# Moving the store of converted weight rows from the sync queue to GpSimd's queue

## The chip, the cores and the metric

The kernel runs on one core of a Trainium2 chip. The core has five engines that run side by side and wait for one another through semaphores: PE (TensorE, matmuls and transposes), DVE (VectorE), ACT (ScalarE), POOL (GpSimd) and SP (SyncE, which here only issues transfers). Each engine takes its instructions strictly in the order in which the program was built. The metric is the device time of one execution in microseconds (us), as the median of a few runs.

## The reference, cut to what matters

Attention with local windows and a few global tokens makes `x` of 2304 rows; a dense layer pair follows; its result goes through a soft mixture of experts.

```python
x = attn_out.transpose(0, 2, 1, 3).reshape(B * S, H * D)   # 2304 x 512
h = x @ w_in                                               # 512 x 2048
g = np.maximum(0.01 * h, h)
y = g @ w_out                                              # w_out: 2048 x 512
logits = y @ phi                                           # phi: 512 x 32
d = softmax of logits over the rows; slot_input = d.T @ y
slot_out = per expert: maximum(slot_input @ w1, 0) @ w2
out = softmax of logits over the columns @ slot_out
```

`w_in` and `w_out` arrive as 64-bit floats, which the kernel reads as pairs of 32-bit words.

## The kernel before

`g @ w_out` is never formed for all rows. The kernel needs `w_out` twice: early as `w_out @ phi` (the tile `pmat`, with which logits come straight from `g`), and late, at about 430 us, as the 32-bit weights that turn the summed rows into `slot_input`. So a phase of the program, from about 75 to 140 us, converts `w_out` in 16 chunks of 128 rows, here called chunk 0 to chunk 15. For each chunk:

- SP loads the raw words into a ring of four buffers (`rraw`, L233; chunks 0 to 3 come in halves into other buffers).
- `convert` makes 32-bit floats: two scalings on ACT (L251 and L250, the second into a fresh buffer `wo`), two bit operations on DVE (L253, L257), an integer add on POOL (L261).
- SP stores `wo` to a scratch tensor `wo_f` in HBM (L338), from where four transfers fetch it back at 324 us (L1063).
- PE transposes `wo` in four pieces (`wotp`, L345), ACT copies the result to `wt` (L347), and PE multiplies it with `phi` (`ptps`, L354). After every fourth chunk the product is copied (DVE, `pv`, L359), transposed (PE, L360) and stored in `pmat` (ACT, L361).

There are three `wo` buffers: L250 of one chunk needs the store and the transposes of the third chunk before it. The one PSUM buffer of `wotp` makes each group of transposes wait for the copy to `wt` of the chunk before.

The same stretch holds other work. Attention for the second batch runs score matmuls (`sc`, L434), masked maxima on DVE (L446), four exponentials for each half on ACT (L454), transposes (`etp`, L473), and the product with the values (`po`, L493; DVE scales it into `xn`, L501). The first dense layer runs matmuls (`hp`, L689), whose results are transposed (`gtp`, L726), copied (`gT`, L728, on ACT or DVE in turn) and multiplied with `pmat` (`lg`, L887). The buffer of `xn` for the second batch lies where the raw and `wo` buffers lay, so L501 also waits for the last stores of `wo`.

What order these have on an engine is decided when the program is built: the code names the pieces in a merged list, and a scheduler that plays the program against its own idea of durations then fixes one order for each engine. A changed instruction can therefore change the order of others.

Of the kernel before, what the change touches and what calls it, by code (L numbers as in the profile page):

```python
# [20 lines left out]
def kernel(  # L21
# [15 lines left out]
    nc = tc.nc  # L37
# [4 lines left out]
    P = 128  # L42
# [27 lines left out]
    with tc.tile_pool(name="id", bufs=1) as idp:  # L70
# [6 lines left out]
        out=s44[:, 0, :], in_=ident.rearrange("p (g s) -> p s g", g=4), axis=AX.X, op=ALU.add  # L77
# [58 lines left out]
    for r in range(2):  # L136
        nc.gpsimd.affine_select(
            out=em4[:, r, :], in_=em4[:, r, :], compare_op=ALU.is_ge, fill=0.0,
# [3 lines left out]
            out=em4[:, r, :], in_=em4[:, r, :], compare_op=ALU.is_ge, fill=0.0,  # L142
# [147 lines left out]
    wo_f = dr.tile([FF, DM], F32, name="wo_f") if w_out.dtype == I64 else w_out  # L290
# [25 lines left out]
    def p_items():  # L316
# [16 lines left out]
        def conv_(c, j):  # L333
            wo = pb.tile([P, 512], F32, tag="wo", name="wo", bufs=3)
            for h in range(2) if c == 0 else (None,):
                wout_s.next(wo if h is None else wo[:, 256 * h:256 * h + 256])
            if wo_f is not w_out:
                nc.sync.dma_start(out=wo_f[512 * j + P * c:512 * j + P * c + P, :], in_=wo)  # L338
            wos.append(wo)

        def chunk(c, j):
# [20 lines left out]

        seq_ = [(c, j) for c in range(4) for j in range(4)]
        items.append((0.0, lambda: conv_(0, 0)))
        for n, (c, j) in enumerate(seq_):
            if n + 1 < len(seq_):
                items.append((0.2, lambda a=seq_[n + 1]: conv_(*a)))
            items.append((0.5, lambda c=c, j=j: chunk(c, j)))
            if j == 3:
                items.append((1.2, lambda c=c: prod(c)))  # L370
# [691 lines left out]
    for n, t in enumerate(wo2):  # L1062
        nc.sync.dma_start(  # L1063
            out=t, in_=wo_f[512 * n:512 * n + 512, :].rearrange("(k p) f -> p k f", p=P)
# [193 lines left out]
    for t0 in range(0, NTT, 4):  # L1258
        n = min(4, NTT - t0)
        pt = bank("sc", "ctp", 2)  # L1260
        for t in range(n):
# [7 lines left out]
            out=dst, in0=dst, scalar=odd, in1=pt[:, 0:P * n], op0=ALU.mult, op1=ALU.add  # L1269
# [21 lines left out]
    for m, (c0, c1) in enumerate(((0, 256), (256, 384), (384, 512))):  # L1291
        W = c1 - c0
        sop = bank(("po", "sm", "tp")[m], "sop", 1 if m < 2 else 2)[:, 0:W]
        for k in range(KF):
# [9 lines left out]
            out=so[:, c0:c1], in0=so0[:, c0:c1], in1=sop, op=ALU.add  # L1304
# [3 lines left out]
        if m == 0:  # L1308
# [3 lines left out]
            out=sst[64:128, c0:c1], in0=sp[64:128], in1=sst[64:128, c0:c1], op=ALU.subtract  # L1312
# [4 lines left out]
        for n, ts in enumerate(order2):  # L1317
# [14 lines left out]
            if len(ts) == 1:  # L1332
# [3 lines left out]
                    out=out.rearrange("(b r) c -> b r c", b=B)[:, 0:SG, c0:c1], in_=ob  # L1336
                )
            else:
# [5 lines left out]
                    out=out[r0:r0 + G * P, c0:c1].rearrange("(t p) c -> p t c", p=P), in_=ob  # L1344
# [36 lines left out]
```

## Time and profile before

| | |
|---|---|
| median of 3 runs | 497.02 us (496.87 to 497.91) |
| the profiled execution | 496.2 us |
| its span, first to last instruction | 494.5 us |
| PE busy | 463.5 us, 94% of the span |
| DVE, ACT, POOL busy | 275.0, 234.3, 160.3 us |
| mean granted clock of TensorE | 0.979 of full speed |

The profiled execution took 1.7 us more than its span. PE is busy nearly all the time, so what matters is the few places where PE stands idle, and whatever adds or removes such a place. Busy time of the other engines counts only where PE waits for them.

### The profile page before, as it was taken

To read this page: it belongs to the slowest core of one execution; us is meant where nothing else is said; L and a number is where in the kernel's file an instruction comes from. 1 tells how busy PE (TensorE), PEld (TensorE's weight loads), DVE (VectorE), ACT (ScalarE), POOL (GpSimd) and SP (SyncE) were. 2 spreads that over 40 slices of the span, in tenths; PEclk is the share of its full clock that TensorE was granted. 3 is DMA by queue.
4 is the path that set the end of the run, shared out by engine and by line. 5 is a ranking of instruction groups with operands and counts; after the bars stand their busy time and mean duration, and the time that the engine had idled before them with its cause. 6 is when DMAs were issued, how large, how long until landed. Compare 5 with 4: busy or idle time off the path is not lost.

```text
span 494.5 us, 13438 instructions
## 1 busy us (share of the span) xinstructions
PE 463.5 (94%) x5323; PEld 322.0 (65%) x5323; DVE 275.0 (56%) x886; ACT 234.3 (47%) x680; POOL 160.3 (32%) x281
## 2 busy tenths in 40 slices
PE   7867889999989999999999999999999999999993
PEld 5645668666766657776777676777777777533463
DVE  4585888498547776556554656427666511413332
ACT  4776899588655345543435444234444432201122
POOL 2044887342400113460615243243667700000000
PEclk9986899999999999999999999999999999999998
DMA  9989598599457655334250231169420079999977
GB/s 177 223 200 267 183 292 313 185 304 311 150 143 144 143 118 93 85 76 129 60 106 1 60 60 45 44 220 405 150 78 2 23 266 357 364 397 371 305 237 214
DMA packets 118362, 90.23 MB, mean 182 GB/s; under 512 B 75356, under 2 KB 100764, under 8 KB 118300
## 3 DMA queue, kind: packets, MB, share of 16 engines
q1 hardware_dynamic: 115628, 88.33, 61.8%
q10 hardware_dynamic: 2672, 1.05, 0.8%
q8 instruction: 42, 0.69, 0.6%
q14 instruction: 20, 0.16, 0.1%
HBM read 76.68 MB, written 8.65 MB: 173 GB/s over the span
## 4 chain that ended last, share of the span: by engine, by line
PE 78%; DVE 4%; ACT 4%; DMA 1%; issue 1%; POOL 0%; ACTq 0%; DVEq 0%; POOLq 0%
PE hp L689 38%; PE gtp L726 4%; PE ehp L1221 3%; PE sc L434 3%; PE up L810 3%; PE po L493 3%; PE lg L740 2%; PE etp L473 2%; PE sop L1297 2%; PE sop L1275 1%; PE gpo L579 1%; PE wotp L345 1%; PE qTp L390 1%; PE kTp L390 1%; PE xtp L659 1%; PE gl L519 1%
## 5 line engine op out<-in xcount | busy, mean ns | idle before, releaser
L689 PE MATMUL hp<-wi,xxh 128*128 128x512 f32 x512 | 167.2, 408 | 1.2 <-ACT xxh L665 1.2
L689 PEld LDWEIGHTS hp<-wi,xxh 128*128 128x128 f32 x512 | 91.8, 190 | 28.2 <-issue 8.2
L717 POOL COPY g<-gb 32x256 f32<-32x256 f32 x206 | 82.7, 401 | 82.6 <-DVE gb L708 55.5
L689 PE MATMUL hp<-wi,xxl 128*128 128x512 f32 x256 | 101.0, 396 | 0.0
L696 ACT ACTIVATE g<-hp 128x512 f32<-128x512 f32 x60 | 35.3, 595 | 56.2 <-PE hp L689 54.2
L454 ACT ACTIVATE se<-se,nmx 128x128 f32<-128x128 f32 x128 | 49.6, 390 | 21.5 <-DVE nmx L452 21.4
L689 PEld LDWEIGHTS hp<-wi,xxl 128*128 128x128 f32 x256 | 48.3, 189 | 12.5 <-issue 1.7
L200 POOL COPY vw<-vw 32x1664 f32<-32x1664 f32 x10 | 15.8, 1575 | 78.3 <-DMA vw<-in_v_g_dram 34.9
L446 DVE CUSTOM_DVE_ANT_0 se<-sc,mask 128x128 f32<-128x128 f32 x128 | 28.9, 284 | 12.1 <-PE sc L434 12.0
L261 POOL TENSOR_TENSOR wn<-wn,rraw 128x512 int32<-128x512 int32 x16 | 22.8, 1435 | 34.5 <-DVE wn L257 33.0
L708 DVE STREAM_TRANSPOSE gb<-g 128x512 f32<-128x512 f32 x32 | 22.2, 702 | 19.3 <-ACT g L696 14.0
L434 PE MATMUL sc<-kw,qT 64*32 64x128 f32 x1024 | 29.2, 283 | 0.8 <-DVE mx L446 0.4
L493 PE MATMUL po<-vw,eT 128*32 128x64 f32 x1024 | 24.2, 232 | 3.5 <-issue 2.1
L261 POOL TENSOR_TENSOR wo<-wo,rraw 128x512 int32<-128x512 int32 x12 | 16.0, 1332 | 31.7 <-DVE wo L257 7.2
L434 PEld LDWEIGHTS sc<-kw,qT 64*32 64x32 f32 x1024 | 19.8, 109 | 8.9 <-issue 5.3
L493 PEld LDWEIGHTS po<-vw,eT 128*32 128x32 f32 x1024 | 18.4, 116 | 10.2 <-issue 7.4
L477 DVE COPY eT<-etp 128x512 f32<-128x512 f32 x28 | 18.7, 684 | 9.9 <-PE etp L473 9.9
L454 ACT ACTIVATION_READ_ACCUMULATOR se<-se,nmx 128x1 f32 x128 | 24.1, 188 | 0.0
L473 PE MATMUL etp<-identr,se 128*128 128x128 f32 x128 | 22.4, 296 | 0.2
L405 DVE COPY kw<-kT 128x672 f32<-128x672 f32 x32 | 19.8, 653 | 3.1 <-ACT kT L394 2.7
L251 ACT ACTIVATE rraw<-rraw 128x512 int32<-128x512 uint32 x28 | 18.7, 673 | 4.3 <-DMA rraw<-in_moe_w_out_dram 3.1
L473 PEld LDWEIGHTS etp<-identr,se 128*128 128x128 f32 x128 | 15.8, 146 | 6.3 <-ACT se L454 2.3
(232 smaller groups left out, 777.9 us busy)
## 6 DMA issues: line engine op xcount, KB each, us to landing
ew<-in_moe_w_dram SPq DMA_DIRECT2D x23, 1024.0 KB, 9.5
rraw<-in_moe_w_in_dram SPq DMA_DIRECT2D x16, 512.0 KB, 5.5
vw<-in_v_l_dram SPq DMA_DIRECT2D x60, 112.0 KB, 3.2
rraw<-in_moe_w_out_dram SPq DMA_DIRECT2D x12, 512.0 KB, 6.7
ew<-in_moe_w_dram SPq DMA_DIRECT2D x9, 512.0 KB, 9.2
ew<-in_moe_w_dram SPq DMA_DIRECT2D x17, 256.0 KB, 5.5
wo_f<-wo SPq DMA_DIRECT2D x16, 256.0 KB, 3.2
vn<-in_v_l_dram SPq DMA_DIRECT2D x4, 1024.0 KB, 6.3
```

The lines of the kernel that those rows point to most:

```text
L261: nc.gpsimd.tensor_tensor(out=di, in0=di, in1=m, op=ALU.add)
L405: nc.vector.tensor_copy(kw[:, :, 0:96], src)
L434: last_a[0] = nc.tensor.matmul(bks[e][32 * u:32 * u + 32, P * T:P * T + P], qt[64 * e:64 * e + 64, 32 * U:32 * U + 32], kw[win(U) // (NW / ...
L446: nc.vector.tensor_tensor_reduce(out=s[:, T, :], in0=bk[:, P * T:P * T + P], in1=mask[:, 0 if T == 0 else 2 if T == NT - 1 else 1, :], sca ...
L454: exp_last[0] = nc.scalar.activation(out=s[:, T, :], in_=s[:, T, :], func=AF.Exp, bias=nmx[:, e, T:T + 1], accum_out=sm[:, T, e:e + 1],).ins
L473: last_a[0] = nc.tensor.transpose(pt[:, P * T:P * T + P], es[e][:, T, :], ident).ins
L493: last_a[0] = nc.tensor.matmul(pov[32 * u:32 * u + 32, T, e, :], ets[e][:, 32 * U:32 * U + 32], vw[:, win(U), e, :], start=True, stop=True ...
L689: nc.tensor.matmul(hp, a[:, k, :], w[c][:, k, :], start=(k == 0 and n == 0), stop=(k == KD - 1 and n == 2),)
L696: nc.scalar.activation(out=gs, in_=hp, func=AF.Prelu, alpha=0.01)
L708: nc.vector.transpose(out=gb[:, f % 2], in_=gs)
L717: copy(dst[32 * c:32 * c + 32, :, a], src[32 * a:32 * a + 32, :, c])
L726: nc.tensor.transpose(pt[:, P * c:P * c + P], g[:, o:o + P], ident)
```

## The change

One call goes to another engine. The store of each converted chunk is issued from POOL, whose add completes the chunk, instead of from SP.

```diff
             if wo_f is not w_out:
-                nc.sync.dma_start(out=wo_f[512 * j + P * c:512 * j + P * c + P, :], in_=wo)
+                nc.gpsimd.dma_start(out=wo_f[512 * j + P * c:512 * j + P * c + P, :], in_=wo)
             wos.append(wo)
```

Sixteen transfers of 256 KB leave SP's queue and stand in POOL's. There each follows the add of its own chunk and waits for that add; only chunks 1 and 2 are stored together, behind the add of chunk 2. No other POOL instruction changes its place. On SP the loads that stood behind a store now follow one another, and some raw loads stand ahead of attention's loads where they stood behind.

The scheduler also puts other engines' work in another order between chunk 8 and chunk 15. In the rows below, one row counts a score or value matmul once where the trace shows it as two.

PE around chunks 8 to 10 (before with -, the change with +): the score matmuls of the second batch's first heads are `sc_1555` and `sc_1556`.

```order
-L345 MATMUL wotp<-identr,wo 128x128 x4
-L434 MATMUL sc_1555<-kw,qT 32x128 x16
+L434 MATMUL sc_1555<-kw,qT 32x128 x15
+L345 MATMUL wotp<-identr,wo 128x128 x4
+L434 MATMUL sc_1555<-kw,qT 32x128
 L390 MATMUL qTp<-identr,qn 128x128 x4
 L360 MATMUL ptps<-identr,pv 128x128
-L345 MATMUL wotp<-identr,wo 128x128 x4
 L434 MATMUL sc_1556<-kw,qT 32x128 x16
-L354 MATMUL ptps<-wt,phis 32x128 x2
+L354 MATMUL ptps<-wt,phis 32x128
+L345 MATMUL wotp<-identr,wo 128x128 x4
```

The transposes of chunk 8 moved behind most of `sc_1555`, those of chunk 9 behind `sc_1556`. Further on, those of chunk 10 moved behind four `hp` matmuls, and those of chunk 11 behind twenty more.

PE at the end of the conversion, from the transposes of chunk 13 on, before:

```order
L345 MATMUL wotp<-identr,wo 128x128 x4
L354 MATMUL ptps<-wt,phis 32x128
L493 MATMUL po<-vw,eT 32x64 x15
L434 MATMUL sc_1981<-kw,qT 32x128 x16
L493 MATMUL po<-vw,eT 32x64 x4
L345 MATMUL wotp<-identr,wo 128x128 x4
L354 MATMUL ptps<-wt,phis 32x128
L493 MATMUL po<-vw,eT 32x64 x7
L434 MATMUL sc_1982<-kw,qT 32x128 x16
L345 MATMUL wotp<-identr,wo 128x128 x4
L354 MATMUL ptps<-wt,phis 32x128 x14
```

And in the change, from the value matmuls just ahead of chunk 13 on:

```order
L493 MATMUL po<-vw,eT 32x64 x9
L345 MATMUL wotp<-identr,wo 128x128 x4
L354 MATMUL ptps<-wt,phis 32x128
L434 MATMUL sc_1981<-kw,qT 32x128 x16
L354 MATMUL ptps<-wt,phis 32x128
L345 MATMUL wotp<-identr,wo 128x128 x4
L434 MATMUL sc_1982<-kw,qT 32x128 x16
L354 MATMUL ptps<-wt,phis 32x128
L345 MATMUL wotp<-identr,wo 128x128 x4
L354 MATMUL ptps<-wt,phis 32x128 x13
L726 MATMUL gtp<-identr,g_860 128x128 x4
L887 MATMUL lg<-gT,pmat 32x128 x3
```

The value matmuls and a block of `hp` that stood between these chunks now stand ahead of chunk 13; chunk 12's transposes moved from ahead of that block to behind it, 16 value matmuls, the transpose L360 and the 9 shown above ahead of chunk 13's. Behind the last `lg` row shown, the change has the second `gtp` of this tile, which before stood ahead of it.

ACT at the same place, before:

```order
L361 ACTIVATE pmat<-ptps 128x128
L250 ACTIVATE wo<-rraw 128x512
L347 COPY wt<-wotp 128x512 x2
L454 ACTIVATE se,sm<-se,nmx 128x128 x4
L347 COPY wt<-wotp 128x512
L454 ACTIVATE se,sm<-se,nmx 128x128 x4
L728 COPY gT<-gtp 128x512 x2
```

And in the change:

```order
L250 ACTIVATE wo<-rraw 128x512
L361 ACTIVATE pmat<-ptps 128x128
L347 COPY wt<-wotp 128x512
L250 ACTIVATE wo<-rraw 128x512
L347 COPY wt<-wotp 128x512
L454 ACTIVATE se,sm<-se,nmx 128x128 x8
L347 COPY wt<-wotp 128x512
L728 COPY gT<-gtp 128x512 x2
```

The last copy to `wt` stood behind the first four exponentials and now stands behind all eight; the first scaling of chunk 15 (the last L250) moved behind the copy of chunk 13. On DVE the second bit operation of chunk 15 (L257) moved behind the four masked maxima of `sc_1981`.

## Rows read from the trace of the kernel before

**Rows 1.** Stretches: start:end, length, busy us of PE, PEld, DVE, ACT, POOL.

```profile
104.00:120.00 16.00, 14.46 (x213) 10.26 (x213) 15.04 (x48) 13.10 (x35) 6.21 (x5) 1.00 1.10 301
131.00:142.00 11.00, 9.36 (x181) 6.91 (x179) 5.09 (x25) 6.70 (x23) 2.59 (x2) 1.00 0.41 121
200.00:300.00 100.00, 100.00 (x1375) 72.38 (x1373) 56.53 (x229) 44.30 (x160) 37.11 (x76) 1.00 0.32 69
```

**Rows 2.** Waits of PE, 60 to 170 us: total, times, longest.

```profile
PE gtp L726 <- DVE gT L728: 1.3, 1, 1.3
PE wotp L345 <- POOL wo L261: 0.7, 1, 0.7
...
PE sc L434 <- DVE mx L446: 0.4, 1, 0.4
```

**Rows 3.** Waits of SP's queue, 60 to 145 us, the longest.

```profile
SPq L338 <- POOL wo L261: 23.0, 10, 3.3
```

**Rows 4.** Instructions on tile wo: shortest/median/longest ns, first and last start.

```profile
L253 DVE TENSOR_SCALAR wo<-wo x20: 280/426/1289, 75.5 to 133.3; 128x512 uint32<-128x512 uint32 x12, 128x256 uint32<-128x256 uint32 x8
L338 SPq DMA_DIRECT2D wo_f<-wo x16: 319/338/1523, 80.7 to 136.9; - x16
L250 ACT ACTIVATE wo<-rraw x12: 660/686/706, 87.9 to 132.6; 128x512 f32<-128x512 f32 x12
L257 DVE SCALAR_TENSOR_TENSOR wo<-rraw,wo x12: 689/692/693, 89.8 to 133.8; 128x512 uint32<-128x512 uint32 x12
L261 POOL TENSOR_TENSOR wo<-wo,rraw x12: 1288/1304/1552, 90.8 to 134.8; 128x512 int32<-128x512 int32 x12
```

**Rows 5.** The stores of line L338, from issue to landing.

```profile
DMA to landing us min/median/max: 2.0/3.2/6.2
```

**Rows 6.** Timeline of SP, the last store: start, length.

```profile
136.91 0.44 SPq L338 DMA_DIRECT2D wo_f<-wo  x1
```

**Rows 7.** Timeline of POOL, two adds; in brackets the idle time ahead.

```profile
117.97 1.31 POOL L261 TENSOR_TENSOR wo<-wo,rraw 128x512 int32<-128x512 int32 x1 [4.17 <-DMA vw<-vw]
...
134.79 1.30 POOL L261 TENSOR_TENSOR wo<-wo,rraw 128x512 int32<-128x512 int32 x1 [2.25 <-DVE wo L257]
```

**Rows 8.** Timeline of DVE, 117.9 to 141.3 us.

```profile
117.99 1.32 DVE L459 TENSOR_SCALAR sm<-sm 128x8 f32<-128x8 f32 x1
...
135.10 0.29 DVE L446 CUSTOM_DVE_ANT_0 se<-sc,mask 128x128 f32<-128x128 f32 x1 [0.62 <-PE sc L434]
...
139.71 0.69 DVE L501 TENSOR_TENSOR xn<-po,rs 128x512 f32<-128x512 f32 x1 [1.07 <-PE ptps L354]
140.32 0.68 DVE L728 COPY gT<-gtp 128x512 f32<-128x512 f32 x1
...
141.11 0.16 DVE L459 TENSOR_SCALAR sm<-sm 128x8 f32<-128x8 f32 x1
```

**Rows 9.** Timeline of ACT at the last chunk.

```profile
136.44 0.40 ACT L454 ACTIVATE se<-se,nmx 128x128 f32<-128x128 f32 x1
...
138.06 0.59 ACT L347 COPY wt<-wotp 128x512 f32<-128x512 f32 x1
```

**Rows 10.** Timeline of PE: chunk 13's transposes, and the end of the stretch.

```profile
132.58 0.66 PE L345 MATMUL wotp<-identr,wo 128*128 128x128 f32 x4
...
142.19 0.42 PE L887 MATMUL lg<-gT,pmat 128*32 128x128 f32 x6
```

**Rows 11.** The chain of waits in order of time: start, length, count.

```profile
126.92 0.99 PE ptps L354 x26
127.91 0.59 PE wotp L345 x4
...
132.15 0.26 PE ptps L360
...
133.53 0.49 PE po L493 x23
134.02 1.01 PE sc L434 x32
```

## The prediction

> **What bounds the kernel now.** I read the stretches first. Between 200 and 300 us PE is busy for 100.00 of 100 us [rows 1], so a delay or a gain made before 150 us goes through to the end, unless a later idle place takes it up. The change sits between 75 and 140 us, and there PE has two stretches that are not full: 104 to 120 us (14.46 of 16 busy, 1.54 idle) and 131 to 142 us (9.36 of 11, 1.64 idle) [rows 1]. The waits of PE say who ended the idle time: chunk 9's transposes waited 0.7 for its add on POOL, score matmuls 0.4 for a masked maximum on DVE, and the transposes of `g` 1.3 for a copy on DVE [rows 2]. The last one is the longest, and it ends the stretch. The reader should see in the timeline of DVE that this copy (140.32) stands right behind L501 (139.71) [rows 8]. L501 waits for the last stores of `wo`, since its buffer lies where theirs lay; the last store was issued at 136.91 [rows 6], 2.8 before L501 starts. The trace puts L501's wait on a `ptps`, but it names only what it sees as the last of several, so I take the store to be a candidate. What a store costs to land is thus not free: the last one stands on the path.
>
> SP waited 23.0 us for POOL's adds, in ten pieces, at the head of its queue [rows 3]. That is idle time of an engine that computes nothing. It matters only if a load behind it is late for someone, and the waits of PE name no load.
>
> **The change part by part.**
>
> *SP loses sixteen issues* of 0.338 each, median [rows 4], about 5.4 us, and the waits ahead of them. For the raw loads, the ring of four buffers demands the same adds as the stores did, so they gain little more than the issue ahead of them; some gain more, because they now stand ahead of attention's loads. I price the whole at nothing on the path. The cover is that no load is waited for by PE; without it the gain would be the idle time of the first place, 1.54 at most.
>
> *POOL gains sixteen issues.* The trace has no transfer issued by POOL. The nearest rows are SP's own issue, 0.319 to 1.523 [rows 4], and POOL's add of the same tile, 1.30; I take 1.0, nearer the add, since POOL works on it as on an instruction. POOL's adds come 4.0 apart on average (90.8 to 134.8, twelve of them [rows 4]), and each takes 1.30, so an issue of 1.0 fits between them: sixteen of them cost nothing, except the last, whose landing is waited for. No add but the next chunk's is queued behind an issue. If an issue took more than 4.0 - 1.3 = 2.7, that cover would be gone and every chunk would slip.
>
> *The store's landing* was 2.0 to 6.2, median 3.2 [rows 5]. A landing frees a `wo` buffer for the scaling (L250) three chunks later, 12 us on less the 3 that lie between L250 and the end of an add, so only the last store is exposed. I take 2.8 for it, the distance read above, because it falls into the same lightly loaded stretch.
>
> On this term the Trainium skill has a figure that no row here shows (DMA: Bandwidth & Descriptors, section "Latency and other measured facts"): the first byte of a transfer moves some 0.6 us after issue from SP's kind of queue and some 1 us after issue from GpSimd's. By it the last store would come 0.4 later than SP's in place of my 1.0, L501 would no longer end last in the walk below, and the sum would be 0.8 in place of 1.2.
>
> *The order of PE, first place.* The transposes of chunks 8, 9 and 10 moved behind score matmuls, so chunk 9's add (wait 0.7) has time, and the wait of 0.4 behind it goes as well: a lead of 1.1. Bounds: all idle time of the stretch, 1.54, and nothing, since on ACT two raw scalings (L251) moved ahead of exponentials and may wait there for their loads. I take 1.1, the two named waits.
>
> *The order at the end of the conversion.* Here I walk the change from the moment T at which chunk 12's transposes start. Before, PE began chunk 13's transposes at 132.58 [rows 10], with thirteen chunks behind it; at T the change has the same work behind it but for chunk 12's transposes (0.59) and L360 (0.26) [rows 11]. So T = 132.58 - 1.1 - 0.59 - 0.26 = 130.6. Prices: four transposes 0.59, a value matmul 0.49/23, sixteen score matmuls 1.01, the big `ptps` 0.99, a small one as 0.26 [rows 11]; L250 0.69, L253 0.43, L257 0.69, the add 1.30 [rows 4]; four masked maxima 4 x 0.29 = 1.16 [rows 8]; four exponentials 138.06 - 136.44 = 1.6, a copy to `wt` 0.59 [rows 9]. From T:
>
> PE: chunk 12's transposes to 0.59, 32 value matmuls to 1.27, L360 to 1.53, 18 more to 1.91, chunk 13's transposes to 2.50, `ptps`, `sc_1981` to 3.77, `ptps`. ACT: copy 12 to 1.25, L250 of chunk 14 to 1.95, `pmat` to 2.2, copy 13 from 2.55 to 3.15, L250 of chunk 15 to 3.85. DVE and POOL: chunk 14's bit operations to 3.1, its add to 4.4; PE waits for it 0.4 and has `sc_1982` done at 6.1. DVE: L253 of chunk 15 to 4.3, the maxima of `sc_1981` to 5.46, L257 to 6.15; POOL's last add to 7.45. PE has waited about 1.1 more and is through chunk 15's transposes at 8.1. ACT: the first exponentials start behind L257 and the negated maxima, 6.4 to 8.0, the second four to 9.6, and only then copy 15, to 10.2. Before, that copy stood between the two fours. So the big `ptps` waits 2.1 and ends at 11.2, the next `gtp` at 11.8, `lg` at 12.2. The last store: add 7.45, issue 1.0, landing 2.8, so L501 runs from 11.25 to 11.95, the copy of `gT` (0.68 [rows 8]) to 12.6, and the `gtp` behind it to 13.2.
>
> The stretch then ends at 130.6 + 13.2 = 143.8. Before, the same work was done at 142.19 + 0.42 = 142.61 [rows 10]. **The sum: 1.2 later.** The profiled execution took 496.2, 0.8 less than the median of 497.02; the difference goes on top of the median: 498.2. Bounds: with the lead at 1.54 and a store that lands at its fastest (0.32 + 2.0), `gtp` is last at 12.8 and the sum is +0.4; with no lead and the slowest (1.52 + 6.2), L501 starts at 15.2, the end is at 17.1 and the sum is +6.1.
>
> *The kernel's end.* ACT's last two output copies and stores swap places; the same two copies and two issues remain, so I price it at nothing.
>
> **The rivals.**
>
> *Faster.* The chunks run ahead because SP is free. Place: 104 to 120 us, price 1.54, with the end of the conversion as costly as before: 495.5. For it: 23.0 us of waits at the head of SP's queue. Against: the ring and the three `wo` buffers tie a chunk to earlier chunks, whoever issues the stores. It decides if chunk 15's add is done 2 us earlier than in the walk, as PE then waits for nothing at the end.
>
> *No change.* Lead and loss cancel: the lead is 1.54 and the last store is quick, +0.4, or a later idle place takes up the rest: 497.4.
>
> *Much slower.* Issuing on POOL is dear, or holds DVE and is held by it. The trace shows such holding between the two engines: an operation on 128x8 numbers took 1.32 beside POOL's add (117.97, 1.31) and 0.16 without one [rows 7, 8]. If each of the last three stores cost the slow end (issue 1.52, landing 6.2), the end would come 6.1 later; I put this case at half of it, 500.1.
>
> The Trainium skill states this holding as a rule (SBUF — State Buffer, section "SBUF: two separate sides"): GpSimd writes the descriptors of its transfers through a port pair that it shares with VectorE, which one of them holds for a whole instruction. The trace agrees for the add, 1.32 against 0.16; for an issue no row shows it.
>
> That the change does not do what it says is excluded: the built order has the sixteen stores on POOL.
>
> **How the numbers follow.** About 0.2%, 1.0 us, is what a measurement of this kernel can tell from no change. The forecast, slower by 1.0 to 2.5, has 0.33; much slower 0.12; no change 0.30; faster 0.25. So slower 0.45, same 0.30, faster 0.25. The likeliest is 498.2; its own range, by the bounds without the slow landing, is 497.4 to 499.3 (no lead, +2.3). The range over the cases goes from a little below the faster rival, 495.2, to beyond the much slower one, 501.2, and leaves out the far ends with about 0.15.
>
> **What would show it.** Right: no wait of PE for POOL at chunk 9; copy 15 behind eight exponentials, and a `ptps` that waits some 2 us for it; L501 3.8 or more behind the last add (before: 139.71 against 136.09 [rows 7, 8], 3.6). Wrong: PE meets no wait between chunks 13 and 15, or stands idle at chunks 8 to 11, or an add stands late behind an issue. The prediction fails most easily at the walk, since a chunk that comes 1 us earlier removes its waits.

## The result, and the profile after

The changed kernel took 502.86 us, median of 4 runs (501.21 to 505.75), against 496.94 (496.32 to 497.91) for the kernel before: ratio 1.0119, 95% interval 1.0072 to 1.0166, some 5.9 us slower. The profiled execution took 503.54, its span 501.8.

The stores first. Their group among the instructions on tile `wo` (shortest, median and longest ns, first and last start):

```profile
L338 POOL DMA_DIRECT2D wo_f<-wo x16: 542/557/744, 83.6 to 141.4; - x16
```

Their time from issue to landing: all sixteen, the one issued at 138.13, and the last, issued at 141.38.

```profile
DMA to landing us min/median/max: 2.3/4.3/6.2
...
DMA to landing us min/median/max: 2.3/2.3/2.3
...
DMA to landing us min/median/max: 3.9/3.9/3.9
```

A store takes POOL 0.56, less than the 1.0 that the prediction took. The landing's median is 1.1 longer than from SP [rows 5], but the store of chunk 14 landed in 2.3, and the last one, 3.2 us behind it, took 3.9. In the kernel before the last one (issued at 136.91) took 2.6:

```profile
DMA to landing us min/median/max: 2.6/2.6/2.6
```

Now the stretches that answer to [rows 1], with one more: start:end, length, busy us of PE, PEld, DVE, ACT, POOL, then the granted clock.

```profile
104.00:120.00 16.00, 14.38 (x255) 10.72 (x252) 14.59 (x49) 13.22 (x36) 7.81 (x8) 1.00 1.07 294
131.00:142.00 11.00, 9.38 (x176) 6.44 (x174) 5.40 (x24) 6.54 (x19) 5.53 (x6) 0.95 0.41 121
142.00:150.00 8.00, 6.34 (x56) 4.44 (x57) 2.42 (x6) 2.97 (x10) 0.00 (x0) 0.50 0.61 154
200.00:300.00 100.00, 100.00 (x1408) 72.92 (x1407) 56.27 (x218) 43.28 (x146) 39.95 (x85) 1.00 0.34 74
```

PE is idle for about as long as before in the first two. The new thing is the granted clock of 0.50 from 142 to 150: TensorE ran at 1.2 GHz instead of 2.4. Before, it was 1.00 from 100 to 400 us. The waits of PE between 60 and 180 us that answer to [rows 2]:

```profile
PE ptps L354 <- ACT wt L347: 1.5, 2, 1.3
PE wotp L345 <- POOL wo L261: 1.1, 2, 0.6
PE sc L434 <- DVE mx L446: 0.8, 2, 0.6
PE sc L434 <- ACT pmat L361: 0.7, 1, 0.7
PE wotp L345 <- ACT wt L347: 0.6, 1, 0.6
...
PE gtp L726 <- ACT gT L728: 0.3, 1, 0.3
```

And the timeline of PE at the end of the conversion, which shows where those waits stand:

```profile
137.88 0.66 PE L345 MATMUL wotp<-identr,wo 128*128 128x128 f32 x4 [0.44 <-POOL wo L261]
139.11 1.08 PE L434 MATMUL sc<-kw,qT 64*32 64x128 f32 x32 [0.56 <-DVE mx L446]
...
141.14 1.12 PE L345 MATMUL wotp<-identr,wo 128*128 128x128 f32 x4 [0.62 <-POOL wo L261]
143.58 1.92 PE L354 MATMUL ptps<-wt,phis 128*32 128x128 f32 x26 [1.32 <-ACT wt L347]
145.83 1.12 PE L726 MATMUL gtp<-identr,g 128*128 128x128 f32 x4 [0.34 <-ACT gT L728]
146.88 0.65 PE L887 MATMUL lg<-gT,pmat 128*32 128x128 f32 x6
147.46 1.12 PE L726 MATMUL gtp<-identr,g 128*128 128x128 f32 x4
```

PE stands idle at chunk 14, at `sc_1982`, at chunk 15 and at the big `ptps`, and from chunk 15's transposes on everything is slow: four transposes take 1.12 instead of 0.66, the 26 `ptps` 1.92 instead of 1.06. On the side of the store, the timeline of DVE:

```profile
137.02 1.10 DVE L253 TENSOR_SCALAR wo<-wo 128x512 uint32<-128x512 uint32 x1 [0.70 <-ACT wo L250]
145.44 0.69 DVE L501 TENSOR_TENSOR xn<-po,rs 128x512 f32<-128x512 f32 x1 [2.18 <-DMA wo_f<-wo]
```

And SP's, around the issue of that store:

```profile
139.97 1.18 SPq L184 DMA_DIRECT2D vw<-vw  x2
141.25 0.63 SPq L185 DMA_DIRECT2D vw<-vw  x1
141.99 0.89 SPq L1109 DMA_DIRECT2D ew<-in_moe_w_dram  x1
```

Here the trace names the store as what L501 waits for, 2.18 us. And SP shows what lies around that store, which POOL issued at 141.38: three copies inside `vw`, a tile in the core's own memory (224, 224 and 208 KB), and a load of 512 KB (`ew`, expert weights). Before, the last store stood ahead of these on SP's own queue.

Part of the difference is chance. For that, one place ahead of the first store and one behind the conversion are enough: the first transposes of the conversion (L345), and the matmuls of L755, which come after the same work in both orders. Before, and in the changed kernel:

```profile
81.04 0.60 PE L345 MATMUL wotp<-identr,wo 128*128 128x128 f32 x4
...
149.24 0.70 PE L755 MATMUL lg<-lp,s 128*128 128x256 f32 x2
```

```profile
83.07 0.69 PE L345 MATMUL wotp<-identr,wo 128*128 128x128 f32 x4
...
156.19 0.70 PE L755 MATMUL lg<-lp,s 128*128 128x256 f32 x2
```

The changed kernel is 2.03 late before it has issued any store. From the one place to the other it takes 73.12 instead of 68.20: 4.92 more. From L755 to the end of the span it is 345.61 against 345.26. So 4.9 of the span's 7.3 us lie in the conversion, and whether the 2.0 ahead of it belong to the change is the first question.

### The profile page after: what moved, and what is told of

Read it like the earlier page. It is cut to its first block, busy times and chain, and to the rows that moved or that the text cites. A ratio compares the mean times of both kernels' runs of the same rounds, so it can differ in the third digit from the quotient of the medians.

```text
span 501.8 us, 13417 instructions
## 1 busy us (share of the span) xinstructions
PE 468.5 (93%) x5323; PEld 325.5 (65%) x5323; DVE 274.6 (55%) x886; ACT 234.1 (47%) x680; POOL 168.2 (34%) x297
## 4 chain that ended last, share of the span: by engine, by line
PE 76%; DVE 4%; ACT 4%; DMA 2%; issue 1%; POOL 0%; ACTq 0%; DVEq 0%; POOLq 0%
PE hp L689 37%; PE gtp L726 4%; PE ehp L1221 3%; PE sc L434 3%; PE up L810 3%; PE po L493 3%; PE lg L740 2%; PE etp L473 2%; PE sop L1297 1%; PE sop L1275 1%; PE qTp L390 1%; DMA rraw<-in_moe_w_out_dram 1%; PE lg L887 1%; PE kTp L390 1%; PE xtp L659 1%
## 5 line engine op out<-in xcount | busy, mean ns | idle before, releaser
L251 ACT ACTIVATE rraw<-rraw 128x512 int32<-128x512 uint32 x28 | 18.7, 675 | 5.0 <-POOL wo L261 2.7
L728 ACT COPY gT<-gtp 128x512 f32<-128x512 f32 x26 | 14.8, 588 | 11.6 <-PE gtp L726 8.3
```

## The experiments

In all but the two repeats the order of PE, ACT and DVE is held by a table (in e13 to e16 that of SP as well): each instruction is tied to the one that stands ahead of it in a given order (an edge for the issue order alone, without a wait), so the store's queue, the order and single rows can be changed one at a time. The helper, with the table cut:

```diff
+def in_order(tc):
+    traced = {i.name: i for i in tc.nc.cur_bb.bb.instructions}
...
+    for rows in ORDER.values():
...
+        for a, b in zip(ns, ns[1:]):
+            tc.add_manual_dep(traced["I-%d" % b], "I-%d" % a, dep, reason="order")
```

All results in one table. "To L755" is the time from the first transposes of the conversion to L755 in the profiled run, as worked out above; "landing" is that of the last store. Each ratio is to the kernel before on the same chip (medians 497.74 to 498.26 there).

| run | median us | ratio, 95% interval | first transposes | to L755 | landing |
|---|---|---|---|---|---|
| kernel before | 496.94 | | 81.04 | 68.20 | 2.6 |
| changed kernel | 502.86 | 1.0119 (1.0072 to 1.0166) | 83.07 | 73.12 | 3.9 |
| e1, changed kernel again | 503.55 | 1.0123 (1.0082 to 1.0163) | 81.35 | 73.22 | 5.2 |
| e4, kernel before again | 498.59 (one run) | | 83.30 | 68.14 | 2.5 |
| e2, GpSimd's queue, old order | 502.26 | 1.0078 (1.0048 to 1.0108) | 83.04 | 73.71 | 3.0 |
| e3, sync queue, new order | 507.67 | 1.0199 (1.0165 to 1.0233) | 80.30 | 76.64 | 4.1 |
| e5, new order, then old | 507.19 | 1.0191 (1.0158 to 1.0224) | 82.95 | 78.36 | 3.0 |
| e6, two rows back | 503.47 | 1.0127 (1.0088 to 1.0166) | 81.92 | 74.20 | 5.0 |
| e7, idle pieces filled | 503.72 | 1.0111 (1.0065 to 1.0157) | 80.84 | 74.11 | 5.9 |
| e8, last four from sync | 502.75 | 1.0103 (1.0078 to 1.0129) | 82.63 | 70.93 | 3.7 |
| e9, no wait for the landing | 502.22 | 1.0084 (1.0058 to 1.011) | 82.22 | 72.32 | not waited for |
| e11, both: e7 and e9 | 500.52 | 1.0041 (1.0016 to 1.0066) | 81.78 | 69.60 | not waited for |
| e12, both: e6 and e9 | 501.83 | 1.0069 (1.0039 to 1.0099) | 79.83 | 71.63 | not waited for |
| e13, ew late | 503.40 | 1.0104 (1.0077 to 1.0131) | 82.61 | 72.96 | 4.6 |
| e16, e7 with ew late | 501.31 | 1.0061 (1.0039 to 1.0082) | 81.23 | 70.74 | 3.6 |
| e14, before with ew early | 502.49 | 1.0097 (1.0066 to 1.0127) | 83.41 | 72.80 | 4.8 |
| e10, before, no wait for the landing | 497.81 | 0.9987 (0.9965 to 1.0009) | 80.79 | 68.17 | not waited for |
| e15, e10 with ew late | 496.11 | 0.997 (0.9949 to 0.999) | 83.08 | 67.84 | not waited for |

**Chance ahead of the first store.** The changed kernel (e1) and the kernel before (e4) once more, unchanged.

> The change once more, as it is. Two losses were seen in its first profile: 2.0 us before the first store (first transposes of the conversion at 83.07 instead of 81.04, with a granted clock of 0.50 from 36 to 52 us), and about 5 us between 131 and 160 us (granted clock 0.50 from 142 to 150). Theory: the second belongs to the change and comes again (clock 0.50 somewhere in 138 to 152 us, the first four gtp behind the last ptps at half speed, 1.1 us instead of 0.66); the first is chance, since no instruction ahead of 80 us was moved, and comes in other sizes: time 500 to 504. Rival: the first belongs to the change as well: the first transposes again at 83 or later, time 503 or more in every run.

> The kernel before once more, for a second profile. Where the early loss is chance, the clock between 36 and 60 us and the start of the first transposes (81.04 in the first profile) differ by some tenths to 2 us; where it belongs to the change, they stay within 0.3 us of the first profile.

The kernel before started its conversion at 83.30 this time, the changed one at 81.35: the early 2 us are chance and change sides. The stretch in which they arise, 36 to 60 us, in the two traces of the changed kernel:

```profile
36.00:60.00 24.00, 18.52 (x229) 13.28 (x222) 16.30 (x45) 18.10 (x49) 13.80 (x11) 0.59 0.80 212
```

```profile
36.00:60.00 24.00, 18.40 (x228) 13.44 (x225) 17.73 (x47) 17.07 (x44) 13.92 (x11) 0.71 0.86 230
```

The granted clock is 0.59 and 0.71, with nearly the same idle time; the kernel before had 0.71 and 0.66. The time to L755 hardly moves: 68.20 and 68.14 before, 73.12 and 73.22 after. So the change costs 4.9 to 5.1 us there in both pairs of traces, and that number tells kernels apart better than their times, which for the kernel before spread from 496.01 to 501.02 on this chip.

**Queue or order.** One half of the change at a time: e2 has the stores on GpSimd's queue and the old order, e3 the stores on the sync queue and the new order.

```diff
 # e2: changed kernel; e3: kernel before
+        in_order(tc)     # ORDER: rows of PE, ACT, DVE as in the kernel before (e2), as in the changed one (e3)
```

> Stores from GpSimd's queue, but TensorE, VectorE and ScalarE are held to the order of the kernel before, instruction by instruction. Theory (the loss is the moved rows' and the halved clock that follows their idle pieces): no PE wait over 1.3 us between 131 and 145 except the one for gT, granted clock 1.0 in 142 to 150; the last store still lands about 1 us later than from the sync queue, so 497 to 498.5. Rival (GpSimd's queue itself is dear: its issues hold POOL and DVE, and its landings are late): the adds stand late and the time stays at 500.5 to 503.

> The other half: stores from the sync queue as before, but TensorE, VectorE and ScalarE are held to the order of the changed kernel. Theory (order): copy 15 behind eight exponentials, the last ptps waits 1 us or more for it, the clock falls to 0.50 between 140 and 150, and the time is 500 to 503. Rival (queue): no idle piece longer than before, granted clock 1.0, 496.5 to 498.

Neither theory holds alone: both halves are slow, at new places. In e2 a scaling waits for a store (waits of ACT, 100 to 120 us: total, times, longest):

```profile
ACT wo L250 <- DMA wo_f<-wo: 2.3, 2, 1.7
```

And the clock falls behind it (a window of e2):

```profile
116.00:130.00 14.00, 14.00 (x101) 10.36 (x101) 12.00 (x43) 11.28 (x41) 5.52 (x6) 0.51 1.01 293
```

In the old order L250 of chunk 10 (at 113.98; an expectation below calls the place chunk 9) stands so early that the store of chunk 7, issued by GpSimd at 107.49 and landing in 6.4, has not landed yet; copies and exponentials wait behind it on ACT. The end of the conversion itself was quiet (clock 1.00 from 130 to 150). The runs of e2 spread over 7.7 us (497.35 to 505.08), and its one trace is of the longest, so how often the clock falls there is not shown. In e3 a raw scaling (L251) that stands earlier in the new order waits for its load, which stands on SP's queue behind a store that waits for an add. PE's waits there, and then the window:

```profile
PE wotp L345 <- ACT wt L347: 3.1, 1, 3.1
```

```profile
104.00:112.00 8.00, 6.24 (x29) 4.52 (x33) 2.52 (x6) 4.49 (x9) 1.28 (x1) 0.58 0.87 224
```

So queue and order belong together: each order fits the queue for which it was laid out, and the loss of the changed kernel is not what either half loses.

**A mixed order.** e5 keeps the stores on GpSimd's queue, takes the new order up to chunk 9 and the old one from there.

> Stores from GpSimd's queue; the order of the changed kernel up to chunk 9 (where the scaling L250 stands late enough for a store of GpSimd's to have landed), and from there on the order of the kernel before. Theory (two orders lose in two places: the old one at chunk 9, where L250 waits 1.7 us for a landing, the new one at chunks 14 and 15): neither place is left, no PE wait over 1.0 us between 105 and 145, granted clock 1.0 from 104 to 150, 498 to 500. Rival (a store from GpSimd's queue lands late for some scaling in any order that is packed as densely as the old one): another L250 waits over 1 us for a landing, the clock falls to 0.50 again, 501 or more.

Neither case came, and this tells nothing of the change. At the seam of the two orders PE waited 2.20 us for a copy to `wt` (at 117.73) and 3.34 for chunk 10's add (at 122.75). That chunk's bit operations (L253 at 120.06) stood on DVE behind a copy of `eT`, which had waited 3.36 for transposes that PE did only behind its first wait; the clock was 0.5 to 0.6 from 116 to 132 us. No landing of a store was part of it.

**One leg at a time.** Four kernels in the new order, stores on GpSimd's queue. e6 puts two rows back where the kernel before has them, in terms of the order:

```diff
 ACT
 L347 COPY wt<-wotp 128x512
-L454 ACTIVATE se,sm<-se,nmx 128x128 x8
-L347 COPY wt<-wotp 128x512
+L454 ACTIVATE se,sm<-se,nmx 128x128 x4
+L347 COPY wt<-wotp 128x512
+L454 ACTIVATE se,sm<-se,nmx 128x128 x4
 DVE
+L257 SCALAR_TENSOR_TENSOR wo<-rraw,wo 128x512
 L446 ISA se,mx<-sc_1981,mask 128x128
...
-L257 SCALAR_TENSOR_TENSOR wo<-rraw,wo 128x512
```

> The changed kernel in its own order but for two rows: L257 of chunk 15 stands ahead of the masked maxima (on VectorE), and copy 15 between the two fours of exponentials (on ScalarE), both as in the kernel before. The last 26 ptps then start some 1.3 us earlier. Theory A (the waits make the loss, the clock adds to it only if PE stands idle long enough): with the wait of 1.3 gone the clock stays at 1.0, 498 to 500. Theory B (the idle pieces of 0.4 to 0.6 ahead of it, at chunks 14 and 15, already take the clock down): 0.50 in 140 to 150 again, only the wait is saved, 501 to 502.5.

Both theories failed: 74.20, a little worse than the changed kernel. Copy 15 came earlier, but `sc_1982` now waited 1.3 us for the maxima that L257 pushed back, the clock was 0.50 from 142 to 150 all the same, and the last store landed only at 145.2.

e7 keeps PE busy in its idle pieces, with small matmuls placed in the order:

```diff
+def fill(nc, pt, identr, c, d, j):
+    for _ in range({1: 7, 2: 16}.get(j, 0) if c == 3 and d == 0 else 0):
+        nc.tensor.matmul(
+            pt[:, 256:512], identr, identr.unsqueeze(1).to_broadcast([128, 2, 128]),
...
```

> The changed kernel in its own order, with 23 matmuls of 256 columns (0.11 us each) on the identity into unused columns of the ptps bank, in PE's idle pieces only: 3 ahead of chunk 14's transposes, 4 ahead of sc_1982, 5 ahead of chunk 15's transposes, 11 ahead of the last 26 ptps. The waits stay as they are, PE is busy in them. Theory (the halved clock is most of the loss): granted clock 1.0 from 134 to 155, gtp at 0.66 instead of 1.12, 498.5 to 500.5. Rival (the waits are the loss and the slow matmuls stand where PE would have waited anyway): same waits, 502 to 504 whatever the clock.

They write into a bank in which a product is being summed, so part of `pmat` is changed; the work is otherwise the same. The clock held where PE was kept busy, and the time did not fall: 503.72, the rival's number, though not with the same waits. Windows of e7:

```profile
134.00:142.00 8.00, 7.43 (x119) 6.06 (x109) 3.94 (x21) 4.89 (x19) 3.71 (x4) 1.00 0.72 171
142.00:146.00 4.00, 1.25 (x16) 0.57 (x10) 1.02 (x2) 1.17 (x2) 0.00 (x0) 1.00 0.47 154
146.00:150.00 4.00, 3.67 (x37) 2.84 (x38) 1.23 (x4) 0.86 (x2) 0.00 (x0) 0.62 0.02 4
```

Its timelines of PE and, in the second fence, of DVE:

```profile
146.32 0.66 PE L726 MATMUL gtp<-identr,g 128*128 128x128 f32 x4 [2.54 <-DVE gT L728]
```

```profile
144.98 0.69 DVE L501 TENSOR_TENSOR xn<-po,rs 128x512 f32<-128x512 f32 x1 [4.12 <-DMA wo_f<-wo]
```

PE is through the big `ptps` sooner and then waits 2.54 for the copy of `gT` behind L501, which waits for the last store; behind that wait the clock falls after all. That gave the theory of two legs of nearly one length: the last store's landing, L501 and the copy of `gT`; and copy 15 behind eight exponentials, with the matmuls behind it at half clock. Cutting one uncovers the other.

e8 sends the last four stores from the sync queue:

```diff
-                nc.gpsimd.dma_start(out=wo_f[512 * j + P * c:512 * j + P * c + P, :], in_=wo)
+                (nc.sync if c == 3 else nc.gpsimd).dma_start(out=wo_f[512 * j + P * c:512 * j + P * c + P, :], in_=wo)
```

> The changed kernel in its own order, but the stores of the last four chunks go out from the sync queue. Theory (the end of the conversion is set by copy 15 behind eight exponentials and by the clock, not by the last landing): L501 starts about 1 us earlier, the waits of PE at chunks 14 and 15 and the halved clock stay, 502 to 504.5. Rival (the prediction's: the last store's landing, through L501 and the copy of gT, ends last): 1.5 us or more faster than the changed kernel, 501 to 502.

502.75, as the theory had it; but L501 came only 0.3 earlier behind the first transposes (144.69 - 82.63 = 62.06 against 62.37), since this store landed late as well, in 3.7, from SP's own queue. To L755 it took 70.93; the clock came back at about 146.5 instead of 151. The gain of 2.2 in this one trace does not show in the median.

**The landing cut.** e9 and e10 open the pool of the raw loads ahead of the pool of `wo`, so that L501's buffer comes to lie over the raw loads; L501 then waits for the last add alone. e11 is e9 with the small matmuls of e7, e12 is e9 with the two rows of e6.

```diff
-    pb = pctx.enter_context(tc.tile_pool(name="pb", bufs=4, side="right"))
+    st = pctx.enter_context(tc.tile_pool(name="st", bufs=2, side="right"))
     actx = ExitStack()
-    st = pctx.enter_context(tc.tile_pool(name="st", bufs=2, side="right"))
+    pb = pctx.enter_context(tc.tile_pool(name="pb", bufs=4, side="right"))
```

> The changed kernel in its own order, with one thing moved in memory: the buffer that L501 writes now lies over the raw loads' buffers instead of over those of wo, so L501 waits for the last add and no longer for the last three stores. Theory of two legs (the end of the conversion has two legs of nearly one length: the last store's landing, L501 and the copy of gT on one, copy 15 behind eight exponentials and the matmuls at half clock on the other): L501 starts 1 us or more earlier, but the second leg stays, so from the first transposes to the first sip it takes 355.5 to 356.5 us (changed kernel 356.4, kernel before 351.1), 502 to 504. Rival (the landing alone is the gate): 352 to 354 from the first transposes, 499 to 501.

> The kernel before in its own order with the same move in memory: L501 no longer waits for the last stores. In the kernel before the transposes of g waited 1.3 us for the copy behind L501. Theory (that wait was for the landing): L501 starts 0.7 us or more earlier, the wait falls to 0.5 or less, 350 to 350.5 from the first transposes to the first sip, 496.5 to 497.5 beside some 498 for the kernel before. Rival (L501 waited for the ptps that the trace names): L501 still starts at the end of the last ptps, no gain.

> Both legs cut at once: the move in memory, so that no landing is waited for, and the 23 small matmuls in PE's idle pieces, so that the clock has no reason to fall (they write into the bank in which the product for the last four chunks is being summed, so part of pmat and what depends on it is changed; the amount of work is not). Theory of two legs: no wait of 2.5 us for gT any more, granted clock 1.0 from 130 to 160 us, 352.5 to 354 from the first transposes to the first sip, 499.5 to 501. Rival (something else in the order holds the stretch): 355 or more.

> The landing cut, and copy 15 and L257 of chunk 15 back in the places that they have in the kernel before; no small matmuls. Theory of two legs: the second leg is 1.4 us shorter and the first is gone. If the pieces of 0.4 to 1.3 us of idle PE still take the clock to 0.50, it takes 354 to 355 us from the first transposes to the first sip (501 to 502); if the clock stays at 1.0, 352 to 353 (499 to 500). Rival: no better than two rows alone, 357.

The landing cut alone gives 0.8 to 0.9 (72.32), the clock held alone nothing (74.11), both together 3.5 to 3.6 (69.60). The windows of e11:

```profile
134.00:142.00 8.00, 7.43 (x109) 5.89 (x112) 4.97 (x23) 5.50 (x20) 3.71 (x4) 1.00 0.67 169
142.00:150.00 8.00, 7.41 (x119) 5.29 (x111) 3.29 (x8) 2.62 (x5) 0.00 (x0) 1.00 0.33 87
```

And its timeline of PE:

```profile
141.78 1.06 PE L354 MATMUL ptps<-wt,phis 128*32 128x128 f32 x26 [0.48 <-ACT wt L347]
143.39 0.66 PE L726 MATMUL gtp<-identr,g 128*128 128x128 f32 x4 [0.55 <-ACT gT L728]
```

To the first `sip` (L1196, near the end of the program) e9 took 356.49 and e11 353.77, both within what the two legs gave; e12 took 355.79, outside both of its cases, with the clock at 0.57 from 138 to 146. (In these three as in several others of the runs, about 1.0 of it is a wait of `qTp` for `kT` near 250 us, which the changed kernel doesn't have and whose cause is open; it lies behind L755.) In e10 L501 came at 57.4 behind the first transposes instead of 58.7, so in the kernel before it did wait for the last store, which the prediction could only take as a candidate. But the gain did not arrive: the wait for `gT` fell only to 0.7, and `po` waited 0.4 for copies of `vw`. These went out no later than before, but landed in 5.4 to 5.9 instead of 3.7 to 4.1: `ew`, which waits for the last stores in this layout, now went out 0.7 ahead of them instead of 2.0. The expected 350 to 350.5 to the first `sip` was 351.1.

**Why the last store lands late.** e13 and e16 move one load, `ew`, behind the next loads on SP's queue (e16 with the small matmuls); e14 moves it the other way in the kernel before; e15 is e10 with `ew` behind the copies of `vw`. In terms of SP's order, e13 and e14:

```diff
 e13, from the changed kernel
 L185 DMA vw<-vw 32x13x128
-L1109 DMA ew<-in_moe_w_dram 128x8x128
 L162 DMA kn<-in_k_l_dram 128x4x64 x2
 L162 DMA qn<-in_q_l_dram 128x4x64 x2
+L1109 DMA ew<-in_moe_w_dram 128x8x128
 e14, from the kernel before
+L1109 DMA ew<-in_moe_w_dram 128x8x128
 L338 DMA wo_f<-wo 128x512
 L177 DMA vw<-in_v_l_dram 32x16x64
 L180 DMA vw<-in_v_g_dram 32x2x64
-L1109 DMA ew<-in_moe_w_dram 128x8x128
```

> The changed kernel in its own order, with one load moved on the sync queue: the 512 KB of ew (L1109) go out behind the next kn and qn, some 14 us later, and no longer beside the last store. Theory (the last store lands late, 3.9 to 5.2 us instead of 2.3 alone, since SP, rid of the stores, issues the copies of vw and ew ahead of it or beside it): the last store lands in 3.5 us or less, L501 starts 1 us or more earlier than 62.3 us behind the first transposes; as the other leg (copy 15, clock) stays, the time falls by 1 us at most, 502 to 503.5. Rival (late because GpSimd issued it): it lands in 4 us or more again.

> The small matmuls in PE's idle pieces (which change part of pmat, as in the run without the move in memory), with L501 waiting for the last store as in the changed kernel, and ew late. Theory: with the clock held, the last store's landing is the only leg left; without ew beside it, it lands 1 us or more sooner than the 5.9 us seen with the small matmuls alone, the transposes of g wait 1.5 us or less for gT instead of 2.5, and lg L755 comes 70 to 72 us behind the first transposes instead of 74.1. Rival: landing and wait as before, 74.

> The kernel before in its own order, with that load moved the other way: ew goes out from the sync queue right ahead of the last store (both wait for the same add). Theory (what lies beside the last store sets its landing, whoever issues it): the last store lands in 4 us or more instead of 2.5, L501 starts 1.5 us or more later, the transposes of g wait 2.5 us or more instead of 1.3, and lg L755 comes 69.5 us or more behind the first transposes instead of 68.2; with a clock that falls, 71 or more. Rival: the last store still lands in 3 us, 68.2.

> The kernel before with L501's buffer away from those of wo (as in e10_before_apart), and ew behind the copies of vw, since its wait for the last stores held these copies up there (po waited 0.4 for vw). Theory: gT comes 0.6 earlier, po waits for nothing: lg L755 67.5 to 67.8 us behind the first transposes instead of 68.2, 0.4 to 0.7 us faster than the kernel before, which its runs can hardly show. Rival: another wait takes the place, 68.1 to 68.3.

e14 shows that a neighbour is enough. The store goes out from the sync queue, 0.5 behind `ew` (timeline of SP):

```profile
140.01 0.43 SPq L1109 DMA_DIRECT2D ew<-in_moe_w_dram  x1
140.50 0.57 SPq L338 DMA_DIRECT2D wo_f<-wo  x1
```

Its landing:

```profile
DMA to landing us min/median/max: 4.8/4.8/4.8
```

The waits of PE from 130 to 155 us, and a window behind them:

```profile
PE ptps L360 <- DVE pv L359: 2.5, 1, 2.5
PE gtp L726 <- ACT gT L728: 1.1, 1, 1.1
```

```profile
146.00:150.00 4.00, 2.91 (x31) 2.17 (x35) 2.00 (x6) 0.28 (x1) 0.00 (x0) 0.77 0.65 138
```

One load of 512 KB is moved ahead of one store, on the queue of the kernel before and in its order, and it takes 72.80 instead of 68.20. Of these 4.6 us, 0.7 arise ahead of the load, at chunk 10 (its transposes come 33.61 behind the first ones instead of 32.90), and their cause is open. The rest follows the load: the store is issued 0.5 later behind it, its landing grows from 2.6 to 4.8, L501 comes 3.5 later in all, and the copy `pv`, behind it and the copy of `gT` on DVE, holds PE for 2.5. The wait of 1.1 ahead of that is for a copy on ACT; before, one of 1.3 for DVE stood there. Behind the wait the clock falls, as in the changed kernel.

e13 says that `ew` is not the only neighbour: without it the last store of the changed kernel still took 4.6, beside the copies of `vw` alone, so its expected 3.5 or less was wrong. What brings these copies there? The loads that they need (L177) wait for the value matmuls that free the buffer of `vw`. Waits of SP's queue from 120 to 150 us, in the kernel before and in the changed one:

```profile
SPq L177 <- PE po L493: 3.5, 1, 3.5
```

```profile
SPq L177 <- PE po L493: 6.8, 1, 6.8
```

The new order has these matmuls ahead of chunk 13, so they end 5.9 us ahead of the end of the last add (135.2 against 141.1) and no longer 0.3 behind it. Rid of the stores, SP only waits longer for them. The two halves of the change, e2 and e3, bear this out (us):

| | loads L177, behind the end of the last add | copies L184, behind the issue of the last store | landing of that store |
|---|---|---|---|
| kernel before: old order, SP's queue | 0.40 | 3.68 | 2.6 |
| e2: old order, GpSimd's queue | 0.49 | 4.25 | 3.0 |
| e3: new order, SP's queue | -6.06 | -2.62 | 4.1 |
| changed kernel: new order, GpSimd's queue | -5.88 | -1.41 | 3.9 |

The order sets what lies beside the last store, whichever queue the store is in. In the old order GpSimd's queue adds some 0.4 to the landing; in the new order it adds nothing that one trace could show. That the copies alone make the landing late is not shown directly: no run keeps the new order and takes them away.

In e16 (the clock held, `ew` late) the store took 3.6, the wait for `gT` was 0.3 instead of 2.5, and it came out at 70.74, within the theory. e15 is faster than the kernel before: 496.11, ratio 0.997 (0.9949 to 0.999). Its trace accounts for 0.36 us of that (67.84 against 68.20, a little outside the expected 67.5 to 67.8; the wait for `gT` stayed at 0.7); the rest of the 1.9 in its median is not accounted for and may be chance of the early stretch.

## Why the prediction was wrong, point by point

The direction was right and the size was not: 1.2 us were forecast and some 5.0 came in the conversion; in the medians 498.2 were forecast, with 501.2 as the end of the range, and 502.86 came. The step that failed is the walk through the end of the conversion: its term for the last store's landing, 2.8 us, was 3.9 and 5.2 in the two traces, and it has no term for the halved clock: from the start of L501 to L755 it took 2.2 and 1.2 us more than the walk and, behind its end, the kernel before have.

*POOL's issue*: taken at 1.0, measured 0.30 of idle time and 0.56. It fitted between the adds, as priced; no add stood late behind an issue.

*SP's sixteen issues*: priced at nothing on the path, and that holds at the end of the conversion: PE waited for none of the loads there, and what SP issued beside the last store was set by the order, as the table above shows. What the prediction missed lies in the moved rows: it counted the value matmuls ahead of chunk 13 as PE's time and did not ask which transfers wait for them.

*The landing*: taken as 2.8 for the last store, "because it falls into the same lightly loaded stretch". The copies of `vw` and `ew` now fell into this stretch, and it was 3.9 in the first trace and 5.2 in the second. The issue was dearer in the walk than on the chip, so from the end of the last add to L501 the whole is 4.35 and 5.67 instead of 3.8. The Trainium skill's figure (DMA: Bandwidth & Descriptors, section "Latency and other measured facts"; first byte 0.4 us later from GpSimd's queue) is about the small part, and the traces agree roughly: alone, a store landed 2.3 after its issue from GpSimd's queue, and 2.0 from SP's [rows 5].

*The first place*: half right. The wait of chunk 9 for its add is gone, but score matmuls waited 0.7 for `pmat` and a group of transposes 0.6 for a copy to `wt`, and chunk 12's transposes began 50.15 behind the first ones; with no lead they would have begun at 132.58 - 0.85 - 81.04 = 50.69 [rows 10, 11], so the lead was 0.5 instead of 1.1.

*The walk*: its order of events came true (the wait for chunk 14's add 0.44 against 0.4, copy 15 behind eight exponentials, the big `ptps` waiting 1.3 against 2.1, L501 4.35 behind the last add where 3.8 or more was asked for). It lacks one wait, of 0.56: `sc_1982` waited for the masked maxima of `sc_1981`, which end at 5.46 in the walk, behind the start that it gives `sc_1982`. The last add ended at 141.09 - 83.07 = 58.02 behind the first transposes, 1.0 later than in the walk (130.6 + 7.45 - 81.04 = 57.0): 0.6 from the lead (50.15 where the walk has 49.56); the other 0.4 is no more than L253 lost, which took 1.10 instead of 0.43.

*The missing term*: the granted clock. Behind L501 the walk has 1.95 us to the end of the second `gtp`; measured were 147.46 + 1.12 - 145.44 = 3.14, at half clock. With the first trace the sum closes: 1.2 forecast, 1.56 because L501 started at 62.37 behind the first transposes instead of 60.81, and 1.19 behind L501, together 3.95, against 148.58 - 83.07 - (142.61 - 81.04) = 3.94 measured. The other 0.98 of the 4.92 come between there and L755, behind the walk's end, where the clock stayed at 0.50 to about 151 us. In the second trace the landing has more of it (L501 at 63.42) and what stands behind L501 less (0.5 and 0.7). That the late landing and the clock stand in for each other is what e7, e9 and e11 show. What is left in e11, 1.4, is put down to the other waits of the new order; no run takes them apart.

*The bounds* did hold 4.9 us (up to 6.1), and were then left out of the range as far ends. *The rivals*: "much slower" gave the better size, 500.1, for a reason that did not come about: no issue held DVE. "Faster" asked for the chunks to run ahead; they did so by 0.5 at chunk 12, but the last add ended 3.0 later behind the first transposes than before (58.02 against 136.09 - 81.04 = 55.05 [rows 7]). *The kernel's end*: from L755 on 345.61 against 345.26, nothing to speak of.

## What to carry to other kernels

When a change lets the scheduler lay out the work anew, ask of every row that moves which transfers wait for it. Here value matmuls moved up, the refill of their buffer moved up with them, and its copies came to lie beside a store that a later operation waits for. If something at the end of a stretch waits for that landing (here because a later buffer lies over an earlier one), take the waiter's start from the slow end of the landings, or lay the buffer elsewhere. And where a walk leaves PE idle in several pieces, as this one did, put the matmuls behind them at half clock into the sum as a case of its own; two legs of one length hide each other, so test them cut together.

## What the runs showed of the hardware

In the changed kernel the granted clock had fallen to 0.50 by chunk 15's transposes (141.14, 1.12 us for four), after idle pieces of PE of 0.44, 0.56 and 0.62 us, and it stayed there to about 151 us, although from 143.58 on PE was busy but for 0.34. It fell at this place in every kernel with the new order's tail whose pieces were not filled (the changed one, e1, e3, e6, e8, e9, e12, e13). With the pieces filled it held (e11, e16; in e7 until PE waited 2.54). With the old order's tail it was 1.00 there throughout (before, e2, e4, e5, e10, e15), but for e14, where it fell behind the waits of 1.1 and 2.5; the wait of 1.30 of the kernel before [rows 2] did not bring it down.

A store issued by GpSimd did not hold VectorE. POOL's timeline at an add and its store, of the changed kernel:

```profile
106.03 1.29 POOL L261 TENSOR_TENSOR wo<-wo,rraw 128x512 int32<-128x512 int32 x1 [1.44 <-DMA qn<-in_q_l_dram]
107.61 0.56 POOL L338 DMA_DIRECT2D wo_f<-wo  x1 [0.30 <-DVE wo L253]
```

DVE's at the same time:

```profile
106.67 0.92 DVE L253 TENSOR_SCALAR wo<-wo 128x512 uint32<-128x512 uint32 x1 [0.68 <-issue]
107.63 0.69 DVE L257 SCALAR_TENSOR_TENSOR wo<-rraw,wo 128x512 uint32<-128x512 uint32 x1
```

L253 beside the add takes 0.92 instead of 0.43, L257 beside the store its usual 0.69. The Trainium skill (SBUF — State Buffer, section "SBUF: two separate sides") says that GpSimd's operations and some of VectorE's lock each other out at a shared port pair, and that a transfer issued from GpSimd can starve while VectorE holds it. The first part agrees with L253's rows; a store that starved was not seen, the late landings are those beside other transfers.
